# Output-weight pieces loaded one unit sooner in the transfer order of a decode-attention kernel

## The chip, the cores and the metric

The kernel runs on one core of one Trainium2 chip. The metric is the device time of one execution in microseconds (us). A profiled execution also has a span, the time between the first and the last thing that its trace records; in these runs the time is 1.7 to 3.1 us longer than the span. The granted clock is the share of its full clock that PE was allowed, as the profile shows it.

Engines are named as in the profile: PE is TensorE (matmuls and transposes), PEld its weight loads, DVE VectorE, ACT ScalarE, POOL GpSimd, SP the sync engine, whose queue (SPq) issues nearly all transfers in program order. The Trainium skill is the set of notes on the chip that this text cites by page.

## The reference, cut to what matters

Two problems, A and B, of decode attention with grouped heads: 4 sequences, one query token, 32 query heads on 8 key/value heads, head size 128. A looks at 8192 cached positions, B at the last 2048.

```python
q = (x @ wq).reshape(B, Sq, Hq, Dh).transpose(0, 2, 1, 3)
k, v = repeat(k_cache, 4, axis=1), repeat(v_cache, 4, axis=1)   # B: only the last 2048 positions
p = softmax(einsum("bhqd,bhkd->bhqk", q, k) * Dh ** -0.5)
o = einsum("bhqk,bhkd->bhqd", p, v)
return o.transpose(0, 2, 1, 3).reshape(B, Sq, Hq * Dh) @ wo     # wo: 4096 x 512
```

Everything is read once: 184.56 MB, nine tenths of it K and V.

## The kernel before

The work is cut into 20 units: units 0 to 3 are the sequences of B, units 4 to 19 are pairs of key/value heads of A. A unit of A has one K load and one V load of 4 MB each. Two units make a turn. K and V have two buffers each, so the load of K for unit u waits for the transposes of unit u-2, and that of V for the value matmuls of unit u-2.

PE works in a fixed order. In unit u it transposes K(u), makes the scores (S), and then does the value matmuls (PV) of unit u-1. The last two of the 16 groups of scores stand behind the first value matmuls; this matters in e10. Each even unit also holds one step of the output projection (OPJ), after about 12 of its 16 groups of transposes:

```python
for k in range(NJ + LA):                    # NJ = 16 groups of transposes, LA = 3
    if k < NJ:     TOK.append(("T", k))
    elif k == NJ:  TOK.append(("SM",))
    else:          TOK.append(("PV", pc)); pc += 1
    if k >= LA:    TOK.append(("S", k - LA))
...                                          # (cut)
AFTER = {("S", 2): ("OT",), ("S", 5): ("OL",), ("S", 8): ("OPJ",)}   # in even units only
```

The projection of turn `tn` needs a piece of the output weights of 1 MB in the buffer `Wo_sb`, of which there is only one:

```python
def pe_job_OPJ(tn):
    ...                                      # (cut) 8 matmuls with Wo_sb as the moving operand
    op("pe", fn, waits=[("E", ol_idx[tn]), ("wo", tn) if tn in pieces else None, bankfree(idx)], inc=("T", idx))
```

There are seven such pieces, for turns 3 to 9. All K, V and output-weight loads are issued by SP, in this order:

```python
kv_load("K", 0)
for u in range(1, NU + 1):                   # NU = 20
    if u < NU:
        kv_load("K", u)                      # waits for the transposes of unit u-2
    kv_load("V", u - 1)                      # waits for the value matmuls of unit u-3
    tn = u // 2
    if u % 2 == 0 and tn in pieces:
        ...                                  # (cut)
        op("sp", dma(Wo_sb..., src), waits=[("T", opj_idx[tn - 1])], inc=("wo", tn))
```

So before, piece `tn` comes behind K(2tn) and V(2tn-1). V of the last unit comes in four chunks (VL), and the last eighth of the output weights has a buffer of its own (`Wl_sb`) and is loaded at the very end.

Of the kernel before, what the change touches and what calls it, by code (L numbers as in the profile page):

```python
# [14 lines left out]
def bass_concat_heads__gqa_block_cached__sliding_block_cached__decode_kernel(  # L15
# [50 lines left out]
    pieces = {T0P + q: (1, q) for q in range(NSEG)}  # L66
# [3 lines left out]
    with ExitStack() as es:  # L70
# [83 lines left out]
        def op(eng, fn, waits=(), inc=None, bump=None):  # L154
            waits = list(waits)
            if not (eng == "pe" and turn[0] is not None):
                waits = [w for w in waits if w is not None]
            plan[eng].append(dict(fn=fn, waits=waits, inc=inc, turn=turn[0], bump=bump))
# [382 lines left out]
        def dma(dst, src):  # L541
            def fn(e):
                return e.dma_start(out=dst, in_=src)  # L543
            return fn
# [159 lines left out]
        for u in range(1, NU + 1):  # L704
            if u < NU:
                kv_load("K", u)
            kv_load("V", u - 1)
            tn = u // 2
            if u % 2 == 0 and tn in pieces:
                P, q = pieces[tn]  # L710
                src = WO[P][q * C * DH:(q + 1) * C * DH, :].rearrange("(g p r) n -> p g (r n)", p=128, r=REP)
                op("sp", dma(Wo_sb[:, :, :, :].rearrange("p g r n -> p g (r n)"), src), waits=[("T", opj_idx[tn - 1])], inc=("wo", tn))
            if u == 16:
                op("sp", dma(out[:, 0, D:2 * D], osb[:, 1, :]), waits=[("ocp", T0P + NSEG - 1)], inc=("out", 1))
# [168 lines left out]
```

## Time and profile before

The time is 444.79 us, the median of three runs (444.08 to 445.81). The profiled run took 447.97 us, with a span of 445.9 us.

| What | Before | Where it is read |
|---|---|---|
| DMA engines busy, whole span | 97.5% | the page's queues |
| Rate, 4 to 88 us, and 88 to 300 us | 419 and 431 GB/s | table of stretches |
| PE busy | 82% | the page's first part |
| PE waits for K of A, for Wo | 25.8 us, 19.5 us | list of waits |
| Wo, issue to landing | 29.6 to 32.3 us | transfers of that tile |

First the page of the kernel before: the two rows of slices that belong to DMA (each slice 11 us; busy tenths, then GB/s), the queue, and the chain of work that ended last.

```profile
DMA  8999999999999999999999999999999999999990
GB/s 342 420 415 421 420 418 420 422 445 417 438 433 429 426 432 433 432 429 426 435 417 438 432 432 431 428 430 426 429 435 438 429 427 429 427 421 441 417 380 13
...
q1 hardware_dynamic: 12944, 184.56, 97.5%
...
DMA Wo_sb<-in_B_wo_dram 28%; DMA Wo_sb<-in_A_wo_dram 20%; PE KT L256 15%; PE OT L304 10%; DMA K_sb<-in_B_k_cache_dram 7%; PE KT L367 6%; PE SB L289 4%; PE SA L289 2%; PE SA L316 2%; PE KT L304 1%; SPq L543 1%; PE SA L663 0%; PE KT L663 0%; DVE M L396 0%; PE SA L642 0%
```

The first rows say that transfers never stop. The Trainium skill, "DMA: Bandwidth & Descriptors" (Specifications), gives a fabric ceiling of 435 GB/s, and the trace's 431 agrees. The chain says something that looks different: 48% of the span is "DMA into Wo_sb", the very transfers that the change moves. The next two views show how both can be true. The list of PE's waits (total, times, longest, in us) and the transfers (count, size, median us from issue to landing):

```profile
PE KT L256 <- DMA K_sb<-in_A_k_cache_dram: 25.8, 8, 4.3
...
PE KT L367 <- DMA Wo_sb<-in_B_wo_dram: 10.2, 4, 3.5
PE KT L367 <- DMA Wo_sb<-in_A_wo_dram: 9.3, 3, 4.1
```

```profile
K_sb<-in_A_k_cache_dram SPq DMA_DIRECT2D x16, 4096.0 KB, 24.5
...
Wo_sb<-in_B_wo_dram SPq DMA_DIRECT2D x4, 1024.0 KB, 31.3
Wo_sb<-in_A_wo_dram SPq DMA_DIRECT2D x3, 1024.0 KB, 29.6
```

A piece of 1 MB takes as long as a load of 4 MB, because it stands behind an estimated 12 MB of older loads (27 us at 430 GB/s). Its own part is 1.05 MB / 430 GB/s = 2.4 us. The chain puts the whole 30 us down to the transfer that PE happened to wait for.

Last, the end of the run: PE in order of time (start, duration, engine, line, operation, out<-in, count, and in brackets the idle time before it and what ended that). L256 are transposes, L367 the projection, L304 value matmuls.

```profile
394.56 3.53 PE L256 MATMUL KT<-identf,K_sb 128*128 128x128 f32 x16 [2.83 <-DMA K_sb<-in_A_k_cache_dram]
...
406.95 2.54 PE L367 MATMUL KT<-Wo_sb,OL 128*4 128x512 bf16 x8 [2.56 <-DMA Wo_sb<-in_A_wo_dram]
...
417.83 1.94 PE L256 MATMUL KT<-identf,K_sb 128*128 128x128 f32 x16
...
435.13 3.44 PE L304 MATMUL KT<-PT,V_sb 128*128 128x64 bf16 x64
```

The line at 394.56 begins unit 18, that at 406.95 its projection, that at 417.83 the last unit, 19. K of unit 19 was issued at 386.82 and landed 29.7 us later, at 416.5.

### The profile page before, as it was taken

What the parts mean: (1) busy time and instruction counts of PE and PEld (TensorE: products, weight loads), DVE (VectorE), ACT (ScalarE), POOL (GpSimd) and SP (SyncE); (2) the same over time, 40 slices, a digit from 0 to 9 for tenths busy, and PEclk for the clock granted to TensorE, in tenths of its full rate; (3) what the DMA queues carried; (4) which work ended last, traced back from release to release, by engine and by line L of the source; (5) the groups of instructions that cost most, each with busy time, mean ns of one, the idle gap of its engine ahead of it and who ended that gap; (6) DMA issues with size and microseconds to landing.
All of it is one profiled execution on the core that took longest, in us unless ns stands there. A gap on an engine that the chain in (4) does not pass through costs nothing.

```text
span 445.9 us, 15650 instructions
## 1 busy us (share of the span) xinstructions
PE 366.7 (82%) x7282; PEld 337.1 (76%) x7282; DVE 210.1 (47%) x472; ACT 184.3 (41%) x183; POOL 21.3 (5%) x56
## 2 busy tenths in 40 slices
PE   0259898998996899679967968797699779977987
PEld 0248798898896779669966968497579659975986
DVE  0034456565563445446634645174445435543651
ACT  1004374374471527235444535263518233633540
POOL 6100000000000000000000000000000000000000
PEclk9999999999998889899989998899989888988998
DMA  8999999999999999999999999999999999999990
GB/s 342 420 415 421 420 418 420 422 445 417 438 433 429 426 432 433 432 429 426 435 417 438 432 432 431 428 430 426 429 435 438 429 427 429 427 421 441 417 380 13
DMA packets 13047, 184.78 MB, mean 414 GB/s; under 512 B 1332, under 2 KB 2408, under 8 KB 4456
## 3 DMA queue, kind: packets, MB, share of 16 engines
q1 hardware_dynamic: 12944, 184.56, 97.5%
q8 instruction: 8, 0.13, 0.1%
q14 instruction: 7, 0.06, 0.0%
q0 software_dynamic: 64, 0.02, 0.0%
q10 hardware_dynamic: 24, 0.01, 0.0%
HBM read 184.56 MB, written 0.01 MB: 414 GB/s over the span
## 4 chain that ended last, share of the span: by engine, by line
DMA 55%; PE 41%; issue 2%; SPq 1%; DVE 1%; ACT 0%
DMA Wo_sb<-in_B_wo_dram 28%; DMA Wo_sb<-in_A_wo_dram 20%; PE KT L256 15%; PE OT L304 10%; DMA K_sb<-in_B_k_cache_dram 7%; PE KT L367 6%; PE SB L289 4%; PE SA L289 2%; PE SA L316 2%; PE KT L304 1%; SPq L543 1%; PE SA L663 0%; PE KT L663 0%; DVE M L396 0%; PE SA L642 0%
## 5 line engine op out<-in xcount | busy, mean ns | idle before, releaser
L256 PE MATMUL KT<-identf,K_sb 128*128 128x128 f32 x1280 | 206.9, 296 | 32.7 <-DMA K_sb<-in_A_k_cache_dram 25.8
L265 ACT ACTIVATE KT_sb<-KT 128x1024 bf16<-128x1024 bf16 x160 | 162.1, 1021 | 146.3 <-PE KT L256 146.1
L256 PEld LDWEIGHTS KT<-identf,K_sb 128*128 128x128 f32 x1280 | 147.3, 149 | 42.6 <-DMA K_sb<-in_A_k_cache_dram 27.2
L264 DVE COPY KT_sb<-KT 128x512 int32<-128x512 int32 x160 | 110.3, 689 | 105.7 <-PE KT L256 104.2
L304 PE MATMUL OT<-PT,V_sb 128*128 128x64 bf16 x2560 | 84.4, 193 | 1.3 <-issue 1.3
L304 PEld LDWEIGHTS OT<-PT,V_sb 128*128 128x128 bf16 x2560 | 78.4, 98 | 1.4 <-issue 1.4
L289 PEld LDWEIGHTS SA<-RQc,KT_sb 128*128 128x128 bf16 x1280 | 56.4, 98 | 3.3 <-ACT KT_sb L265 0.8
L443 ACT ACTIVATE PT<-Dt 128x1024 bf16<-128x1024 f32 x20 | 21.1, 1057 | 86.3 <-DVE Dt L434 86.3
L289 PE MATMUL SA<-RQc,KT_sb 128*128 128x16 bf16 x1280 | 56.3, 170 | 0.0
L289 PE MATMUL SB<-RQc,KT_sb 128*128 128x16 bf16 x1280 | 55.8, 170 | 0.0
L289 PEld LDWEIGHTS SB<-RQc,KT_sb 128*128 128x128 bf16 x1280 | 52.0, 97 | 1.3
L367 PE MATMUL KT<-Wo_sb,OL 128*4 128x512 bf16 x80 | 26.0, 483 | 19.5 <-DMA Wo_sb<-in_B_wo_dram 10.2
L396 DVE TENSOR_REDUCE M<-SB 128x8 f32<-128x512 f32 (+1 forms) x20 | 13.8, 692 | 43.4 <-PE SB L289 43.4
L367 PEld LDWEIGHTS KT<-Wo_sb,OL 128*4 128x4 bf16 x80 | 7.2, 97 | 32.0 <-issue 27.4
L417 POOL PARTITION_ALL_REDUCE MB<-M1m x20 | 7.7, 385 | 393.9 <-DVE M1m L410 393.9
L187 PE MATMUL KT<-ident,x_sb 4*128 4x4 bf16 x8 | 0.5, 170 | 19.3 <-POOL identf L505 19.3
L187 PEld LDWEIGHTS KT<-ident,x_sb 4*128 4x128 bf16 x8 | 0.4, 112 | 19.5 <-issue 19.5
L434 DVE TENSOR_TENSOR Dt<-SA,MBm 128x512 f32<-128x512 f32 x20 | 13.8, 692 | 0.7
L434 DVE TENSOR_TENSOR Dt<-SB,MBm 128x512 f32<-128x512 f32 x20 | 13.6, 681 | 0.0
L396 DVE TENSOR_REDUCE M<-SA 128x8 f32<-128x512 f32 (+1 forms) x20 | 13.6, 680 | 0.0
L316 PE MATMUL SA<-PT,onesb 128*128 128x64 bf16 x336 | 13.3, 193 | 0.0
L379 DVE TENSOR_TENSOR oacc<-KT,oacc 4x512 f32<-4x512 f32 x4 | 2.7, 680 | 18.4 <-PE KT L367 18.4
(68 smaller groups left out, 123.1 us busy)
## 6 DMA issues: line engine op xcount, KB each, us to landing
K_sb<-in_A_k_cache_dram SPq DMA_DIRECT2D x16, 4096.0 KB, 24.5
V_sb<-in_A_v_cache_dram SPq DMA_DIRECT2D x15, 4096.0 KB, 30.1
K_sb<-in_B_k_cache_dram SPq DMA_DIRECT2D x16, 1024.0 KB, 21.6
V_sb<-in_B_v_cache_dram SPq DMA_DIRECT2D x16, 1024.0 KB, 21.6
V_sb<-in_B_wq_dram SPq DMA_DIRECT2D x1, 4096.0 KB, 12.3
V_sb<-in_A_wq_dram SPq DMA_DIRECT2D x1, 4096.0 KB, 21.6
Wo_sb<-in_B_wo_dram SPq DMA_DIRECT2D x4, 1024.0 KB, 31.3
Wo_sb<-in_A_wo_dram SPq DMA_DIRECT2D x3, 1024.0 KB, 29.6
```

The source lines that it names most:

```text
L256: ins = pe.transpose(out=bkf[:, pi * 128:(pi + 1) * 128], in_=K_sbf[:, slot, t0:t0 + 2, :].rearrange("p t d -> p (t d)"), identity=identf[ ...
L264: return e.tensor_copy(out=KT_sb.bitcast(I32)[:, tj % NKT, :], in_=bkf.bitcast(I32)[:, :])
L265: return e.activation(out=KT_sb[:, tj % NKT, :], in_=bk[:, :], func=ACTF.Copy)
L289: ins = pe.matmul(out=stb[:, t % NTH * C:(t % NTH + 2) * C], lhsT=ktv[:, pi, :, e], rhs=RQc[:, u % 2, t // TS, e, :], start=(e == 0), stop ...
L304: ins = pe.matmul(out=otb[:, s * NW:(s + 1) * NW], lhsT=V_sb[:, slot, t, :], rhs=PT[:, slot, t * C:t * C + NW], start=(j == 0), stop=(j == ...
L316: ins = pe.matmul(out=SA[u % 2][:, s * NW:(s + 1) * NW], lhsT=onesb[:, :], rhs=PT[:, u % 2, c0:c0 + NW], start=(i == 0), stop=(i == n - 1))
L367: ins = pe.matmul(out=bk[0:Bn, 0:D], lhsT=OL[:, i // REP, i % REP, :], rhs=Wo_sb[:, i // REP, i % REP, :], start=(i == 0), stop=(i == C - 1))
L396: return dve.tensor_reduce(out=M1[:, h * n:(h + 1) * n].rearrange("p (s h) -> p s h", h=C), in_=bank[:, :].rearrange("p (s j h) -> p s h j ...
L417: return pool.partition_all_reduce(MB[:, 0:n], M1m[:, 0:n], channels=128, reduce_op=ReduceOp.max)
L434: return dve.tensor_tensor(out=Dt[:, h * NTH * C:(h + 1) * NTH * C].rearrange("p (s j h) -> p s j h", s=Sh, h=C), in0=bank[:, :].rearrange ...
L443: return act.activation(out=PT[:, u % 2, 0:NT * C], in_=Dt[:, :], func=ACTF.Exp, scale=scale)
L543: return e.dma_start(out=dst, in_=src)
```

## The change

The intent is that PE should not stand still in mid-unit for a small piece: each piece is put one unit sooner in SP's order, before K(2tn) and V(2tn-1) instead of behind them.

```diff
-            tn = u // 2
-            if u % 2 == 0 and tn in pieces:
+            tn = (u + 1) // 2
+            if u % 2 == 1 and tn in pieces:
                 P, q = pieces[tn]
                 ...
                 op("sp", dma(Wo_sb..., src), waits=[("T", opj_idx[tn - 1])], inc=("wo", tn))
```

Nothing is added or removed on any engine; only SP's order differs.

## The prediction

> **What bounds the kernel now.** The input transfers do. The DMA view gives 97.5% mean busy share of the 16 engines for the one queue that carries 184.56 MB. In stretches of 4 us, DMA is at about 1.0 from 4 us to 432 us, at 416 to 422 GB/s while the B caches load and about 430 GB/s afterwards, with no dip. The Trainium skill, "DMA: Bandwidth & Descriptors" (Specifications), gives 435 GB/s as the ceiling of the fabric; the trace sits on it. PE is busy 82% and waits for data.
>
> The chain of waits seems to say something else: DMA into Wo_sb is 48% of the span. Those are seven transfers of 1 MB that land 29.6 to 32.3 us after issue. At 430 GB/s 1 MB is 2.4 us; the rest is standing behind older transfers. The chain names the waiter's transfer, not a removable cost.
>
> **What the change does.** No bytes or instructions are added or removed. Seven Wo pieces go ahead of one K and one V load (8 MB, about 19.5 us) and land that much before their use. Their wait for the previous output projection becomes live: it ends mid-unit, before the last transposes that the next K load waits for, so it should block nothing. Data outstanding then is an estimated 16 to 20 us of transfer (from landing delays of 22 to 37 us), so the queue doesn't run dry.
>
> **Gains and losses.**
> - PE's wait for Wo (list of waits: 19.5 us in 7 times) goes to about zero. The K load behind it lands 2.4 us later, so PE waits for K instead: 25.8 us there should become 40 to 47 us. Six of seven pieces only swap one wait for another.
> - The end is different. K for the last unit is issued at 386.8 and lands 29.7 us later, at 416.5, in either order, as the same bytes precede it. PE gets to it only at 417.83, because it waited 2.56 us for Wo (to 406.95) and then ran at a granted clock of 0.57 from 408 to 412. The skill, "TensorE: Matmul & The Clock Gate" (Part 1), has the clock halved after an idle window of about 3.4 us; 0.50 to 0.6 after these waits agrees. With the change, K of the last-but-one unit lands at about 397 instead of 394.5; 9.8 us of transposes bring PE to 406.8, and the rest of the unit at full clock takes about 9.5 us (114.05 to 123.5 in an unstalled turn) instead of 10.9: 416.3. So the last unit starts at about 416.6 instead of 417.8.
> - From there to the end (28 us, PE and DVE, no data waited for) nothing changes. V of the last-but-one unit lands at 426.2, wanted at 427.5; the last output weights land by 438, wanted at 440.2.
>
> **Prediction.** 1.2 us less: 443.6 us, 8 in 10 between 442.2 and 445.4. Faster by over 2%: 0.02; within 2%: 0.96; slower by over 2%: 0.02.
>
> **What would show it.** DMA rate and end of the transfers (432 to 436 us) as before; waits for Wo gone, waits for K grown by about as much; Wo landing 20 to 25 us after issue; the granted clock low after the longer waits for K, not in mid-unit; the last unit's transposes starting 1.2 us earlier; the chain running through K or V loads instead of Wo.
>
> **What would make it wrong.** If Wo's live wait holds back the K load, DMA shows stretches below 0.9 and the time rises by several us. If the queue was in fact short of outstanding data, earlier K issues raise GB/s and the gain exceeds 2 us. If longer waits for K cool PE's clock so that the last two units run slower, the 1.2 us are lost.

## The result, and the profile after

After: 445.03 us, the median of four runs (444.88 to 445.56); before, 444.55 in the same comparison. The ratio is 1.0009, 95% interval 0.9986 to 1.0031. (Ratios here are the mean time of one kernel's fast runs over that of the other's fast runs of the same rounds, so not quite the ratio of the medians.) Executions over 1.5% slower than the fastest of the same kernel are left out of the means. The time lies in the predicted range, but the predicted 1.2 us (a ratio of 0.9973) are not there. The two traces, however, differ by 3.4 us: span 442.5 after against 445.9 before. So the first thing to explain is that the traces disagree with the timings.

The page, the waits, and the transfers of the kernel after:

```profile
DMA  8999999999999999999999999999999999999993
GB/s 335 424 416 424 417 418 421 421 455 398 455 402 449 429 429 424 436 435 429 427 438 435 427 427 424 429 416 444 435 429 425 431 442 432 424 427 429 432 401 107
...
DMA K_sb<-in_A_k_cache_dram 43%; PE KT L256 28%; DMA K_sb<-in_B_k_cache_dram 7%; PE OT L304 5%; PE SA L289 4%; PE KT L367 4%; PE SB L289 3%; PE KT L304 1%; PE SA L316 1%; SPq L543 1%; PE KT L346 0%; PE KT L328 0%; PE SA L663 0%; PE KT L663 0%; DVE M L396 0%
```

```profile
PE KT L256 <- DMA K_sb<-in_A_k_cache_dram: 48.8, 9, 7.7
```

```profile
K_sb<-in_A_k_cache_dram SPq DMA_DIRECT2D x16, 4096.0 KB, 27.7
...
Wo_sb<-in_B_wo_dram SPq DMA_DIRECT2D x4, 1024.0 KB, 19.4
Wo_sb<-in_A_wo_dram SPq DMA_DIRECT2D x3, 1024.0 KB, 20.0
```

No wait for Wo is left, and the chain has lost its 48%. It has got 43% of "DMA into K_sb" for them. PE's waits for K and Wo of A were 25.8 + 10.2 + 9.3 = 45.3 us before (41.9 in e1, a second trace of the same kernel) and are 48.8 us after: the wait moved from one transfer to the next. The transfers run as before.

PE at the end, after:

```profile
396.57 3.67 PE L256 MATMUL KT<-identf,K_sb 128*128 128x128 f32 x16 [7.18 <-DMA K_sb<-in_A_k_cache_dram]
...
406.68 1.89 PE L367 MATMUL KT<-Wo_sb,OL 128*4 128x512 bf16 x8
...
416.01 1.96 PE L256 MATMUL KT<-identf,K_sb 128*128 128x128 f32 x16
...
433.32 2.04 PE L304 MATMUL KT<-PT,V_sb 128*128 128x64 bf16 x64
```

K of unit 19 landed at 416.0 (issued at 384.49, 31.5 us), and unit 19 began there. That is 1.8 us sooner than in the trace of before. The other 1.6 us of the 3.4 lie in the last 10 us, where the 64 value matmuls take 2.04 instead of 3.44 us. No instruction there was changed; the granted clock was different, 0.71 before and 1.00 after. (After the stretch and its length, the columns are the busy time and count of PE, PEld, DVE, ACT and POOL, then the granted clock, the DMA share and GB/s. The first line is of before, the second of after.)

```profile
435.10:441.00 5.90, 5.90 (x145) 5.80 (x144) 0.63 (x2) 0.00 (x0) 0.00 (x0) 0.71 0.05 17
```

```profile
432.00:440.00 8.00, 7.23 (x164) 5.82 (x164) 0.92 (x4) 0.55 (x2) 0.00 (x0) 1.00 0.36 122
```

Whether the new order makes the fast case likelier is left open below.

### The profile page after: what moved, and what is told of

Same layout as the page of the kernel before. It is cut to its first block, busy times and chain, and to the rows that moved or that the text cites. A ratio compares the mean times of both kernels' runs of the same rounds, so it can differ in the third digit from the quotient of the medians.

```text
span 442.5 us, 15650 instructions
## 1 busy us (share of the span) xinstructions
PE 359.4 (81%) x7282; PEld 336.2 (76%) x7282; DVE 209.8 (47%) x472; ACT 184.5 (42%) x183; POOL 21.3 (5%) x56
## 2 busy tenths in 40 slices
DMA packets 13047, 184.78 MB, mean 418 GB/s; under 512 B 1332, under 2 KB 2408, under 8 KB 4456
## 4 chain that ended last, share of the span: by engine, by line
DMA 49%; PE 47%; issue 2%; SPq 1%; DVE 1%; ACT 0%
DMA K_sb<-in_A_k_cache_dram 43%; PE KT L256 28%; DMA K_sb<-in_B_k_cache_dram 7%; PE OT L304 5%; PE SA L289 4%; PE KT L367 4%; PE SB L289 3%; PE KT L304 1%; PE SA L316 1%; SPq L543 1%; PE KT L346 0%; PE KT L328 0%; PE SA L663 0%; PE KT L663 0%; DVE M L396 0%
## 5 line engine op out<-in xcount | busy, mean ns | idle before, releaser
L256 PE MATMUL KT<-identf,K_sb 128*128 128x128 f32 x1280 | 208.9, 298 | 55.9 <-DMA K_sb<-in_A_k_cache_dram 48.8
L256 PEld LDWEIGHTS KT<-identf,K_sb 128*128 128x128 f32 x1280 | 149.7, 151 | 63.7 <-DMA K_sb<-in_A_k_cache_dram 49.9
L367 PE MATMUL KT<-Wo_sb,OL 128*4 128x512 bf16 x80 | 18.9, 379 | 0.0
L187 PEld LDWEIGHTS KT<-ident,x_sb 4*128 4x128 bf16 x8 | 0.4, 113 | 19.4 <-issue 19.4
L367 PEld LDWEIGHTS KT<-Wo_sb,OL 128*4 128x4 bf16 x80 | 6.0, 84 | 8.1
L316 PEld LDWEIGHTS SA<-PT,onesb 128*128 128x128 bf16 x336 | 11.1, 97 | 0.0
## 6 DMA issues: line engine op xcount, KB each, us to landing
Wo_sb<-in_B_wo_dram SPq DMA_DIRECT2D x4, 1024.0 KB, 19.4
```

The source lines that it names most:

```text
L256: ins = pe.transpose(out=bkf[:, pi * 128:(pi + 1) * 128], in_=K_sbf[:, slot, t0:t0 + 2, :].rearrange("p t d -> p (t d)"), identity=identf[ ...
L316: ins = pe.matmul(out=SA[u % 2][:, s * NW:(s + 1) * NW], lhsT=onesb[:, :], rhs=PT[:, u % 2, c0:c0 + NW], start=(i == 0), stop=(i == n - 1))
L367: ins = pe.matmul(out=bk[0:Bn, 0:D], lhsT=OL[:, i // REP, i % REP, :], rhs=Wo_sb[:, i // REP, i % REP, :], start=(i == 0), stop=(i == C - 1))
```

## The experiments

The theory: the transfers set the pace. Away from the end, PE's waits are slack that moves about; at the end, the time is the landing of the last K load plus a fixed piece of PE and DVE work, and what else differs between traces is the draw of PE's clock (what a run happens to be granted). Rivals: PE's waits for Wo cost time (the reading of the chain); or the gain seen in the traces is real and hidden in the time outside the span.

This table has the end of every profiled run (us). Landing is issue plus the time to landing; it is left out for runs in which the last K came in pieces, as the transfer view then gives a median over the pieces.

| Run | Last K lands | Unit 19 begins | Span | Span minus begin |
|---|---|---|---|---|
| before | 416.5 | 417.83 | 445.9 | 28.1 |
| after | 416.0 | 416.01 | 442.5 | 26.5 |
| e1 before again | 416.2 | 416.18 | 444.2 | 28.0 |
| e2 after again | 416.1 | 416.99 | 443.5 | 26.5 |
| e3 last piece only | 416.2 | 416.79 | 443.3 | 26.5 |
| e4 half of Wo | 407.5 | 407.50 | 434.0 | 26.5 |
| e5 six late | 417.3 | 420.98 | 449.0 | 28.0 |
| e6 last late | 413.4 | 428.04 | 456.1 | 28.1 |
| e7 quarters, before's order | | 420.93 | 448.4 | 27.5 |
| e8 quarters, after's order | | 415.65 | 450.8 | 35.2 |
| e9 halves, before's order | | 417.98 | 444.8 | 26.8 |
| e10 halves, after's order | | 411.57 | 446.0 | 34.4 |
| e11 after, PE filled | 416.2 | 416.39 | 444.0 | 27.6 |

### e1: the kernel before, unchanged

No edit.

> The kernel before, unchanged, as a null test with a second profile. Theory A (the profiled run of before was a slow draw of one kernel: it took 447.97 us where the timed runs have a median of 444.55): the new trace is 1 to 3 us shorter than 445.9, with the last unit's transposes starting before 417.8 or with the 64 last value matmuls at full clock (2.0 instead of 3.4 us). Theory B (the trace was typical and the gain of the change is hidden elsewhere, for example in the time outside the span): the new trace has a span of 445 to 446 again and the same cold stretches. Ratio to before: 1.000 within 0.002 for both.

Measured: ratio 1.0013 (0.9986 to 1.0039), and a span of 444.2 us. PE at the end of this second trace of the same kernel:

```profile
394.19 3.67 PE L256 MATMUL KT<-identf,K_sb 128*128 128x128 f32 x16 [5.32 <-DMA K_sb<-in_A_k_cache_dram]
...
406.56 1.89 PE L367 MATMUL KT<-Wo_sb,OL 128*4 128x512 bf16 x8 [1.44 <-DMA Wo_sb<-in_A_wo_dram]
...
416.18 1.96 PE L256 MATMUL KT<-identf,K_sb 128*128 128x128 f32 x16
...
433.43 2.85 PE L304 MATMUL KT<-PT,V_sb 128*128 128x64 bf16 x64
```

This run waits for Wo too, 1.44 us instead of 2.56, and then runs the projection at full speed (1.89 us instead of 2.54). Unit 19 begins at 416.18, as its K lands. The 1.3 us that the first trace lost there, and that my prediction counted as the gain of the change, are absent although nothing was changed. Across the three sets of rounds, and e1 itself, 39 runs of this kernel have spans from 442.2 to 445.8 us. The trace that I predicted from, at 445.9, is longer than every one of them, though one comes within 0.1 us. The three sets ran on three chips, and on each of them the spans of before lie between 442.2 and 445.4 us; the chip of the first trace is not on record.

### e2 and e3: the change again, and the last piece alone

e2 has no edit. e3 moves only the piece of turn 9:

```diff
-            tn = u // 2
-            if u % 2 == 0 and tn in pieces:
+            tn = (u + 1) // 2 if u == 17 else u // 2
+            if (u == 17 or (u % 2 == 0 and u != 18)) and tn in pieces:
```

> The change, unchanged, timed to better than half a per cent. My prediction of 1.2 us less means a ratio of 0.9973; the first four runs said 1.0009 (0.9986 to 1.0031). Theory A: 0.999 to 1.001, that is, the 1.8 us by which the last unit starts earlier in the two traces is mostly the draw of the run. Theory B: about 0.997.

> Only the piece for turn 9 is loaded one unit sooner, the six others stay. If what counts is the end (prediction), this has all of the change's effect: the last unit's transposes start as K lands, near 416, waits for Wo remain 6 times (about 16 us), and the time equals the change's within 0.2%. If all pieces counted (the waits for Wo, 19.5 us, as a cost on the path), it would have a seventh of the effect. With an effect near zero, the profile has to tell: start of the last unit's transposes, and granted clock in the last 30 us.

Measured: e2 0.9994 (0.9973 to 1.0014), e3 0.9990 (0.9969 to 1.0012). Both agree with zero and with each other, within 0.2%; a gain of a tenth of a per cent can't be excluded, and the predicted 0.27% lies at the edge of e2's interval, inside e3's, and outside that of the first rounds. The rival of a gain hidden outside the span falls as well: in e2's rounds the mean span is 443.6 us for the change and 443.9 for before, and the mean times are 2.0 and 2.1 us above these. In e2 unit 19 begins 0.85 us after its K landed: PE had waited 7.86 us for the K of unit 18 and ran it slowly at first. So the change has a draw of its own, at another place. e3 kept six waits for Wo (17.1 us in all) and was not slower than the change, which has none.

### e4: half of the bytes of Wo

```diff
-  op("sp", dma(Wo_sb[:, :, :, :].rearrange("p g r n -> p g (r n)"), src), ...)
+  op("sp", dma(Wo_sb[:, 0, :, :].rearrange("p r n -> p (r n)"), src[:, 0, :]), ...)
```

Its output is wrong, which doesn't matter for the time.

> Order as before, but only half of each Wo piece is loaded (3.67 MB less; a wrong result on purpose). If the bytes bound the kernel (theory), the time falls by 3.67 MB / 430 GB/s = 8.5 us, to about 436 us, ratio 0.981, although each wait for Wo gets only about 1.2 us shorter. If PE's waits for Wo were the cost (rival, as the chain of waits reads), it would fall by what the waits lose: 7 times at most 1.2 us at one end, or not at all if the landing delay of some 30 us stays as it is; the landing delay should stay near 29 us, as it is standing in the queue.

Measured: 435.51 us, ratio 0.9778 (0.9754 to 0.9802), so 9.9 us less than before's mean. K of unit 19 lands at 407.5, 8.7 us before that of e1, where the bytes alone say 8.5; the rest is the end of the profiled run at full clock (26.5 instead of 28 us in the table). The landing delay of the pieces stayed: the last one took 31.0 us.

```profile
PE KT L256 <- DMA K_sb<-in_A_k_cache_dram: 33.3, 10, 5.3
...
PE KT L367 <- DMA Wo_sb<-in_B_wo_dram: 4.9, 4, 1.3
...
PE KT L367 <- DMA Wo_sb<-in_A_wo_dram: 1.2, 3, 0.6
```

Alone, e4 does not tell the theory from its rival: the waits for Wo fell too, from 16.0 us in e1 to 6.1, which is as much as the time. It takes the change beside it: removing 3.67 MB gains what 3.67 MB take; removing 19.5 us of waits without a byte less, as the change does, gains nothing. The two together settle what bounds the middle of the run.

### e5 and e6: pieces later instead of sooner

e5 puts the pieces of turns 3 to 8 behind K(2tn+1), half a unit later; e6 does so with the piece of turn 9 alone.

```diff
...                                     # (cut) the load of a piece becomes a function, wo_load(tn)
+            late = tn < 9              # e6: tn == 9
+            if u % 2 == 1 and tn in pieces and late:
+                wo_load(tn)            # between K(u) and V(u-1)
             kv_load("V", u - 1)
-            if u % 2 == 0 and tn in pieces:
+            if u % 2 == 0 and tn in pieces and not late:
```

> Six pieces (turns 3 to 8) are loaded later instead of sooner, behind the next K load (some 10 us later); the last stays as before. Theory (away from the end the transfers set the pace, PE's waits are slack): PE waits for Wo grow, from 19.5 us to perhaps 40 us, waits for K shrink by about as much, DMA stays at 1.0 and 430 GB/s, and the time stays within 0.5% of before (445 us), although six waits have become much longer. Rival (a wait of PE for Wo costs time): 6 times up to 10 us more, 465 us or above. Also slower, by the theory, if K issues come so late that the queue runs dry; I estimate about 5 us of transfer left at that moment.

> Only the last piece (turn 9) is loaded behind the last K load; the six others as before. Theory (only the end has no slack): Wo lands near 416.5, PE resumes there instead of at 406.8, the last unit starts near 426 instead of 416 to 418, and the time grows by 8 to 10 us, to about 454 us (ratio about 1.02). Rival (all seven waits count alike): a seventh of what the six late ones cost, or nothing.

e5 measured: 452.03 us, ratio 1.0151 (1.0108 to 1.0194). I had expected 0.5% at most, so this was a miss. The waits of the profiled run:

```profile
PE KT L367 <- DMA Wo_sb<-in_B_wo_dram: 30.2, 4, 11.2
...
PE KT L367 <- DMA Wo_sb<-in_A_wo_dram: 12.0, 2, 6.2
...
PE KT L256 <- DMA K_sb<-in_A_k_cache_dram: 3.8, 1, 3.8
```

The waits for Wo grew by 42.2 - 19.5 = 22.7 us, and those for K shrank by 25.8 - 3.8 = 22.0 us. The exchange holds nearly one to one, but it has now used up all the slack that there was. PE ends up behind the data: unit 19 begins 3.7 us after its K landed. Besides, the queue got short: between 88 and 300 us the rate is 426 GB/s instead of 431, with dips (311 from 256 to 260 us), and the last K lands at 417.3 instead of 416.2 to 416.5. So the slack in front of PE is real and finite, about 25 us over the run.

e6 measured: 456.92 us, ratio 1.0251 (1.0211 to 1.0290).

```profile
416.08 3.57 PE L367 MATMUL KT<-Wo_sb,OL 128*4 128x512 bf16 x8 [12.23 <-DMA Wo_sb<-in_A_wo_dram]
...
428.04 1.94 PE L256 MATMUL KT<-identf,K_sb 128*128 128x128 f32 x16
```

One late piece at the end costs 11 us; six late ones before it cost 7. Here nothing can absorb the wait: 12.23 us of it move the begin of unit 19 from 416.2 (e1) to 428.0. I had put it at 426, because I had not counted that PE comes out of such a wait at half speed (the projection takes 3.57 instead of 1.89 us). The wait also holds up the value matmuls for which the next loads stand in line: between 424 and 428 us no byte is moved.

### e7 and e8: K of A in quarters

Could the end be made sooner? In both, PE may begin a unit when a quarter of K is there.

```diff
-            op("sp", dma(buf[:, slot, :, :]..., src), inc=(kind, u, 0))                  # K of A, 4 MB
+            for q in range(NSEG):                                                        # 4 x 1 MB
+                op("sp", dma(buf[:, slot, q * TS:(q + 1) * TS, :]..., src_q), waits=w, inc=("Kq", u, q))
...
-            waits=[("K", u) if k == 0 else None, bankfree(idx)]
+            waits=[("Kq", u, k // 4) if k % 4 == 0 else None, bankfree(idx)]
```

> Order of before; each 4 MB K load of problem A is split into four of 1 MB with a semaphore each, so PE can begin a unit when a quarter has landed. Theory: the last-but-one unit begins 7 us sooner but then stands at the projection until Wo lands near 406.5, so the last unit still begins near 416, and the time stays within 0.3% of before. Waits for Wo grow to 40 us or more.

> The change with the same split of K. Theory: nothing stands in the way of the early start any more; the last-but-one unit's value matmuls wait for V at 406.3, the last unit begins near 411.5 instead of 416 and is then held by the last value chunks (435.5) and the last output weights (437.1). The end comes near 440.5 to 441 in the span, that is 1.5 to 3 us less than before and the change: ratio 0.993 to 0.997. If the start of the last unit was not what bounded the end, the ratio is 1.000 as in the run with before's order.

Both missed. e7: 452.21 us, ratio 1.0167 (1.0124 to 1.0209); e8: 451.98 us, ratio 1.0138 (1.0098 to 1.0178). The stretch from 88 to 300 us, before and in e7 (last three columns: granted clock, DMA share, GB/s):

```profile
88.00:300.00 212.00, 183.25 (x3592) 169.59 (x3589) 108.48 (x234) 97.14 (x96) 6.58 (x22) 0.94 1.01 431
```

```profile
88.00:300.00 212.00, 181.37 (x3601) 165.29 (x3597) 108.42 (x235) 95.49 (x95) 6.75 (x22) 0.94 1.01 425
```

The DMA engines are just as busy and move less. The page counts 19959 packets instead of 13047 for the same bytes. A rate lower by 1.4% is worth an estimated 5 us over A's loads (1.4% of 350 us), which is most of the loss. That the smaller rows are the cause (8 KB instead of 32 KB in a partition) is an inference: the B loads, which have rows of 8 KB in every version, run at 419 GB/s. In e7 the wait for the last Wo was 6.55 us, so the early start was lost there, as the theory said; all waits for Wo made 36.3 us, where 40 or more were expected. In e8 there was no wait for Wo, and PE stood still for V instead, 31.6 us in all. The extra semaphores seem to have a price too: PE runs its program as a loop over turns, at whose end it corrects each semaphore that it waits for, and this step took 2.14 us instead of 1.2.

### e9 and e10: only the last two K loads, in halves

The same idea with most of the costs taken off: 8 MB of the 184 are touched, and each unit waits for two K semaphores, not four.

```diff
+            if kind == "K" and u >= L - 1:          # L = 19
+                for h in range(2):                  # 2 x 2 MB, a semaphore for each half
+                    op("sp", dma(buf[:, slot, h * NTH:(h + 1) * NTH, :]..., src_h), inc=("Kq", u, h))
+                return
```

> Order of before; only the last two K loads are split, into halves of 2 MB with a semaphore each (each unit now waits for two K semaphores; the first can be met 5 us sooner in the last two units). The rate of the transfers should stay at 430 GB/s, as 8 MB of 184 are in smaller pieces. Theory: the last-but-one unit begins sooner but still stands at its projection until Wo lands near 406.5, so the last unit begins near 416 to 418 and the ratio is 1.000 to 1.003 (two more semaphores a turn cost PE's loop up to 0.5 us).

> The change with the same split of the last two K loads. Theory: with Wo already there, the last-but-one unit ends when V has landed (406.3) and its value matmuls are done, the last unit begins near 412 instead of 416.2, its last value work waits for V at 425.9 and for the last chunks (435.5), and the end comes 1 to 2 us sooner: ratio 0.995 to 0.998. This would be the version that beats both. If it is not below 0.999, the end is bound by something after the last K load that I have not named.

e9: 447.67 us, ratio 1.0045 (1.0019 to 1.0072), slightly above the expected band; the rate is 430 GB/s again. As expected, PE starts unit 18 at 390.81, then waits 7.95 us for Wo, and unit 19 begins at 417.98. e10: 448.07 us, ratio 1.0048 (1.0027 to 1.0069): a loss of half a per cent where a gain was expected, although its first half went just as the theory said.

```profile
406.69 0.64 PE L304 MATMUL OT<-PT,V_sb 128*128 128x64 bf16 x16 [1.06 <-DMA V_sb<-in_A_v_cache_dram]
...
411.57 1.97 PE L256 MATMUL KT<-identf,K_sb 128*128 128x128 f32 x16 [0.58 <-DMA K_sb<-in_A_k_cache_dram]
...
426.18 1.03 PE L304 MATMUL OT<-PT,V_sb 128*128 128x64 bf16 x16 [3.47 <-DMA V_sb<-in_A_v_cache_dram]
...
428.33 4.40 PE L304 MATMUL OT<-PT,V_sb 128*128 128x64 bf16 x96
...
435.37 3.38 PE L304 MATMUL KT<-PT,V_sb 128*128 128x64 bf16 x64
```

Unit 19 begins at 411.57, 4.4 us sooner than after the change. Then PE catches up with the next load: V of unit 18 lands at 426.2, and PE waits 3.47 us for it. The last two groups of scores of unit 19 stand behind that wait, so that by its exponential nothing of the 4.4 us is left (ScalarE starts it at 431.63 us, in the change at 431.49). After the wait the granted clock is 0.69 (426 to 435 us), and the value matmuls behind it take 4.40 us (2.96 in the change) and the last ones 3.38 (2.04). The early start is spent on a wait, and then clock is lost as well. What had been hidden behind the last K is the next transfer in line.

### e11: filling PE's gap at the end

```diff
+        def pe_warm(pe):                            # 5 matmuls 128x512 into a free bank, result unused
+            ...
+        op("pe", pe_warm)
         op("pe", pe_seed, waits=[("ocp", NTURN - 1), ("otr", L - 1)])
```

> The change, with five matmuls of no use (128x512, into a free bank) put into PE's gap before the last unit's value matmuls, some 1.1 us. Theory (part of the spread between runs is PE's clock in the last 10 us): the 64 value matmuls take 2.0 us in the profiled run, the slow draws (3.4 us) no longer appear, and the times spread less than the 444.7 to 446.5 of the change; mean ratio 0.997 to 1.000. If the spread stays, it comes from elsewhere, for example from the landing of the last K.

Measured: 446.39 us, ratio 1.0021 (0.9999 to 1.0043), outside the expected 0.997 to 1.000, with times from 445.78 to 447.94. The last value matmuls are at full clock in the trace (2.04 us), but so are they in both traces of the change without it, so this shows nothing about the clock. The spread did not shrink. My filling also came too late: PE was idle for 1.29 us at the end of its loop all the same, and the five matmuls then stood in front of the real work.

```profile
432.82 1.03 PE L647 MATMUL KT<-K_sb,ident 128*128 128x512 bf16 x4 [1.29 <-DVE OT_sb L478]
433.78 0.59 PE L642 MATMUL SA<-oacc,identf 4*4 4x256 f32 x2
```

No version was found that beats both kernels.

## Why the prediction was right or wrong, point by point

**"The input transfers do" bound the kernel: right.** e4 shows it: 3.67 MB less moved the last K by 8.7 us, where bytes over rate say 8.5. The rate and the end of the transfers did not move with the change.

**"The chain names the waiter's transfer, not a removable cost": right.** The change took all 48% of Wo out of the chain and the time stayed; K took its place with 43%.

**"Six of seven pieces only swap one wait for another": right, with a limit.** 45.3 us of waits became 48.8 (50.6 in e2), a little above the predicted 40 to 47 for K alone. e5 shows the limit: when 22.7 us more of waits for Wo had eaten the 22.0 us of waits for K, PE fell behind.

**"It should block nothing": right.** SP now waits 122.4 us for the projections, and DMA still shows no stretch without work; the K load of unit 18 was issued at 369.46, between the two runs of before (371.79, and 368.75 in e1). Wo landed 19.4 to 20.0 us after issue (medians), just below the predicted 20 to 25.

**"1.2 us less": this is the step that failed.** The prediction put it as "PE gets to it only at 417.83, because it waited 2.56 us for Wo (to 406.95) and then ran at a granted clock of 0.57". It is true of that run, and not of the kernel: in e1 the same code waited 1.44 us, ran the projection at full clock and got to the last K as it landed, at 416.18. The term of 1.2 us is 0 in e1 and 1.3 in the first trace. That the range held the result, 445.03 us, is owed to its width and not to this step.

The warning was in the data before any experiment: the profiled run took 447.97 us where the three timed runs had 444.08 to 445.81. A trace that is 3 us longer than the median has 3 us in it that the typical run doesn't have, and a gain of 1.2 us read from it can be a part of those.

**"From there to the end (28 us) nothing changes": half right.** The data were there, as said, but the 28 us are a draw as well. In the table the piece is 26.5 us in the change, e2, e3 and e4, whose first 64 of the last value matmuls take 2.04 us, and 28.0 to 28.1 in before, e1, e5 and e6, where they take 2.85 to 3.44. Whether the change itself makes the second kind rarer, these traces can't tell: e7 and e9, and also e4, keep before's order and show 2.04 us too. That before's fastest runs (span 442.2) are of the 26.5 kind fits 416 + 26.5 = 442.5, but none of those was profiled in full, so it is argued, not shown. The record has a hint: of the nine of the 39 runs with a mean granted clock of 0.953 or 0.954, seven have a span of 442.5 us or less, of the other thirty only one.

**PE's clock.** The Trainium skill, "TensorE: Matmul & The Clock Gate" (Part 1), says that the clock is halved after an idle window of about 3.4 us, and that the window runs freely, so that the outcome varies from run to run. The traces agree with the second statement: in the first trace, four waits for Wo of 2.51 to 2.62 us were followed by projections of 1.89, 1.89, 2.54 and 3.57 us, which is anything from full to half speed. With the first statement they agree only for long waits (12.23 us in e6, then 3.57); the clock also fell in waits well under 3.4 us, in e1 in one of 2.39 us (granted clock 1.00 from 279 to 280 us, 0.50 from 281 to 282). Here the measurement decides. As predicted, the low clock of unit 18 is at its start after the change (3.67 us for the first transposes) and no longer at the projection (1.89). I cited this page in the prediction and used it for one trace only; its second statement, that it is a draw, is what I should have used.

**What stays open.** Whether the change gains about a tenth of a per cent is below what these rounds can tell (0.9994 and 1.0009, each with 0.2% either way). Whether it narrows the spread also stays open: its six runs in the rounds of e2 lie between 444.71 and 446.48 us, before's eleven of the same rounds between 444.31 and 447.18.

## What to carry to other kernels

When the transfers run at their ceiling all the time, moving a small load ahead of a large one only changes which load the engines wait for; the chain of waits shows the name of the last load in line, not a cost. Ask for each wait what the engine will meet next if it ends sooner (here K, and behind K, V), and look for a gain only where nothing stands behind it, or in fewer bytes. Before reading a gain of a few tenths of a per cent from one trace, compare the profiled run's own time with the timed runs, and take a second trace of the same kernel.

## What the Trainium skill lacked or had wrong

- "DMA: Bandwidth & Descriptors" (Specifications and Bandwidth) lists about 358 GB/s as the limit of HBM for a core and says in a note that this side binds for loads from HBM. The same section has 425 GB/s measured with one core running alone, and says that 358 is what each core gets when both of a pair stream. The note leaves this condition out. Here one core sustained 431 GB/s from HBM over 212 us, so for a kernel on one core the fabric's 435 is the number to plan with.
- The same page (Bandwidth) advises transfers of at least 1 MiB for 75% of the peak, from single transfers. For a stream of loads issued by SP it has one figure, in its section on the iDMA fabric: 408.7 GB/s with 1 MiB for each DMA and rows of 4 KiB, not checked by its own words. It lacks larger rows and loads. Here, standing one behind another, loads of mostly 1 MB with rows of 8 KB ran at 419 GB/s, loads of 4 MB with rows of 32 KB at 431, and a mix of both at 425 (4 to 88 us, and 88 to 300 us, before and e7). The last 3% goes with the size of the rows or the loads; which of the two was not separated.
- "TensorE: Matmul & The Clock Gate" (Part 1) states the penalty of the clock gate as under 1% of a typical span; what reached the time at the end here is within that (28.1 against 26.5 us, 0.4% of the span). Its idle window of about 3.4 us is longer than the waits in which the clock fell here (2.39 us in e1). It says that the slow durations vary between runs of one kernel, and lacks what this does to a comparison: the first trace and e1, two of one kernel, differ by 1.7 us in span, of which 1.3 us lie between the begin of the projection and unit 19, where the first ran at a low clock.
- No page that I read has the cost of a PE loop's step to the next turn: 1.2 to 1.3 us idle here, 1.5 to 1.6 with two more semaphores, and 2.14 with six more.
